# Float32 identity matmuls for the last three squarings, seven layer norms on GpSimd, and new orders throughout, in a two-layer attention and state-space kernel

## The chip, the cores and the metric

The kernel runs on one core of a Trainium2 chip. A core has five engines with an instruction queue each: TensorE (PE in the profile, its weight loads PEld), VectorE (DVE), ScalarE (ACT), GpSimd (POOL) and SyncE (SP), which here only issues DMAs. Each queue is worked off in order, and an instruction that has to wait holds up all that stand behind it. The metric is the device time of one execution in microseconds (us).

## The reference

The input `x` is 2048 rows of 512 columns in bf16. Four residual steps follow one another: attention, state-space convolution, attention, convolution, each on the layer norm of `x`. Both attention steps use the same weights, and so do both convolutions.

```python
# attention: 32 heads of 16; each row looks at 8 rows, 0, 2, ... 14 back
qkv = layernorm(x) @ wqkv
attn = softmax(q . k[s - 2w] * scale)        # masked where s - 2w < 0
x = x + (attn . v[s - 2w]) @ wo
# convolution: a kernel of 2048 taps for each of the 512 channels
P = exp(dt*A * l)                            # l = 0 .. 2047, complex, 128 states
K = einsum("dn,dnl,dn->dl", C, P, dt*B).real
x = x + irfft(rfft(layernorm(x)) * rfft(K)) + layernorm(x) * Dskip
```

## The kernel before

The work runs in six stretches, and each has an order written out by hand as a string of letters or tokens. Each letter takes the next call of its list, so the string fixes in which order every engine's queue gets its instructions.

**Front of the first attention and the taps of K (`k_gen`, ORDERK; 0 to 109 us).** The taps are built from powers of z = exp(dt A). `cur[0]` holds z as two float32 planes (real, imaginary) of 128x512. Eleven squarings give z^2 to z^2048. Squaring k takes three instructions (lines 1082 to 1090):

- `s`, `square(k)`: ACT squares both planes of `cur[k]` into `ws`.
- `i`, `double(k)`: DVE forms the new imaginary plane, 2 re im.
- `i` again, `differ(k)`: DVE subtracts the two planes of `ws`: the new real plane. `sq_z`, the tile of the result, has two buffers.

`b` (`power`, `power_neg`) makes bf16 copies of each power on ACT, for the table `B_t` (k = 0 to 2 and 8 to 11) or for `pow_t` (k = 3 to 7), which `c` completes by DMA. `C` (six DVE instructions, `c_part`) forms C times B. `M` (36 DVE instructions, `b_part`) multiplies powers to fill `B_t`; its last products need power 9 (512) and power 10 (1024). `T`, `U` and `H` build four tables `A_t`, two buffers in turn: a head (ACT copies it, for table 0 DVE) and then levels of DVE products from 256 to 4096 elements. `p` multiplies `A_t` with `B_t` on PE, and `x` copies the products to `kgs` on ACT. `G` and `w` make sine constants on ACT, among them `s_Wp` and `s_WpJ`, from which GpSimd makes the masks `Wp` and `WpJ` (line 696).

Between these stand the letters of the first attention's front. Its rows come in four blocks of 4x128 rows (`x_blk`, two buffers). `a` sums rows and squares on ACT for blocks 0 to 2, `3` takes statistics on DVE for block 3, `l` and `W` make the factor `ln_rstd` and the offset `ln_nb` of each row, and the norm itself is in place (lines 193 and 195): `y` on ACT for blocks 0 to 2, `z` on DVE for block 3. `t` transposes a block on PE (line 1194) and `e` copies it to `xnT` on ACT; `k` and `q` are the projections on PE (line 1204), `K` and `Q` their copies on ACT to `kT_ext` and `qT`.

The PSUM has eight banks. Four belong to `pst`, the pool of the first transposes, and four to the front (`la.front_psum`); when `p` starts, `pst` closes and the products `pk` take its banks.

**First attention (CORE0; to about 185 us).** `m` is the DVE product of queries and keys (`prod`, 4096 elements, 2.2 us each), `l` its sums on PE, `x`, `e`, `r`, `n`, `T` the softmax, `P` the product with the values on DVE (`pav`), `S` or `V` its sums on PE in two forms, `O` the output projection, and `a` and `f` the next norm on DVE or ACT. `A` to `H` copy the taps to `k_perm`, on the engine that KROWS names. GpSimd makes the sine arguments `g_i` and `k_perm` (lines 727 and 728).

**First convolution (ORDER0), its end with the second front (ORDERF), second attention (CORE1), second convolution (ORDER1).** `K` and `U` are the first transform step of taps and rows (copies to `a1s`), `k` and `u` the second (`kn`, `kf_sb`, `kf_nat`, `ub`), `m` the product on DVE (`t`), `y` or `Y` the first inverse step in two PE forms, `z`, `v` and `w` the last one, with the residual sum in `x_sb`. The letter behind a token names the engine of its copy: A for ACT, D for DVE. In ORDERF `h` is a layer norm's statistics on half rows, `a`, `p`, `n` the rest of the norm, `T` and `E` transposes and their copies, `P` and `Q` projections.

Of the kernel before, what the change touches and what calls it, by code (L numbers as in the profile page):

```python
# [11 lines left out]
ALU = mybir.AluOpType  # L12
# [33 lines left out]
ORDERK = """  # L46
sCiibsCbiisCiiMbMCGMiMsabiMcbiasMbbCCaGiMMTsibGGTGTicMbGsbiaTbcisbbTTTMGiiTbTiMaGsaGGTMiGacMabTl
MlMMMWMlaiMsiMayMwMiMybyaTMysteMMqatMaaMkeMadTkqMialKMMlQMkWMlaqMMcbqykTQHqUaUKqQaakUTyqUkyqUUpU
KUkyUapxUxtaUpatpeUaldHQqeUqkKUkl3TT33TQkkxpWl3KxTpTxyxTylTWTpqlkyyTqpHKkzkQzxKUtkUktezUqqeUKTkT
kQKztktkTeeKkUkUKTTkkKUUUkUxUUpxEUpkxpUkUUkpEKkKqxpkUxoxpEoKXqUokUkQUpKxpZxXxZXZ  # L50
"""
ORDER0 = """
KD KA KA KA KD KA KD KA KD KA KD kA kD kA kA kD UA KD UA UD kA UA kD UA KD UA
UD UA KD kA u UD m UA KA u UD u UD m KA u kA m m UA u u kD m m u
UA u UD kA m UA kD kA u m kA kD u kA yA m YD m u m u YA u u m u
yA m m u yA m m YA yA yD yD
"""
LATE0 = "a s t g r b m"
ORDERF = """
yA yA z01D yA z00D yA yD h00 yA h01 YA v100A v110A v102A v013A h10 a0 p0 n0G z02A v111A v101A S v112A  # L60
h02 h11 T0 E00A a1 E01A z13D p1 n1G v003A P03 Q00 h12 a2 P01 T1 E10A p2 P00 E11D n2G h03 P11 P12
P13 T2 E20A h13 a3 E21D P02 p3 n3D P22 P21 P10 T3 E30D E31D P23 P20 x1
"""
ORDER1 = """
UA UD UA UD UA UA UD UA UD UA UD u UD u u UA m u m u m UA m u m u
UD m m UA u m u m u u yA YA u m m u yD m YA m u u m m u yA
YA m yA YD w000D yA yA yD yA z03D yA w010D yA yD yA z02D v103A v113D v112D v102D v110D v100A v111D v101A
"""

CORE0 = """  # L70
vvmvvlvmvvmlvxlemvrmnlqmqvlTvqlxevqmlvmvmPvvP1rnllxS0qTmqOeVmrqP4qSl2OPPSOSOPSmPP5On3l8ml6SPCOOV
AlxSPP7eOSrObSPn9POSdOESOPSPbDadBPfaGOtFOaaawVfHSbatO
"""
CORE1 = """
0m1l2ml3mvvqqlmmlmvqqvvllxmemqvlrnvvlmxTqqlvvmqlmvPvvvvmvqlleqVPrmxqmnqSTOePlPmSOPllSPOSPrOSnOPS
mOSPOblxOSPPdeOSrffbVPdfwOnPfVOPSOSPafbOPSdafftOSafatO
"""
ROWS0 = (0, 2, 1, 3, 4, 5, 6, 7, 8, 9, 10, 11, 12, 13, 14, 15)
ROWS1 = (0, 2, 1, 3, 4, 5, 6, 7, 8, 9, 10, 11, 12, 13, 14, 15)
NCOL = (2, 2)  # L80
KROWS = "ADDAADAA"
VROWS = (*range(0, 16, 2), *range(1, 16, 2))
# [912 lines left out]
def k_gen(tc, nc, a_consts, ins, kd, la, x_v, lnst, zero, b_consts):  # L995
# [3 lines left out]
    with ExitStack() as ctx:  # L999
# [6 lines left out]
        sp = c_small.enter_context(tc.tile_pool(name="kg_small", bufs=1))  # L1006
        pst = c_psum.enter_context(tc.tile_pool(name="kg_ps_t", bufs=4, space=PSUM))
        late = {}
        iotas, a_rest = a_consts(sp)
        ident = la.c["ident"]  # L1010
        la.front_open()
        la.front_psum()
        xb, ln, lvar, xps, pps = {}, {}, {}, {}, {}
# [19 lines left out]
        def turned_by(name, rhs):  # L1033
            pt = pst.tile([P, 4, P], F32, name="pt")
            for t in range(4):
                nc.tensor.matmul(pt[:, t, :], lhsT=raw[name][:, t, :], rhs=rhs(t), start=True, stop=True)
            return pt[:].rearrange("p g q -> p q g")
# [11 lines left out]
        dtd = sp.tile([P, 4, P], BF16, name="dt_diag")  # L1049
        nc.vector.tensor_tensor(dtd[:], ident[:].unsqueeze(1).to_broadcast([P, 4, P]), pdt[:, 0, 0:4].unsqueeze(2).to_broadcast([P, 4, P]), ALU.mult)  # L1050
        by_dt, plain = (lambda t: dtd[:, t, :]), (lambda t: ident[:])
        keys()
# [19 lines left out]
        for f in head:  # L1072
            f()
        T = {name: turned_by(name, by_dt if name[0] == "C" else plain) for name in ("B_re", "B_im", "C_re", "C_im")}
        for name, copy in (("B_re", nc.scalar.copy), ("B_im", nc.scalar.copy)):
# [4 lines left out]
        nc.vector.tensor_tensor(cur[0][:, 0], a_re, cs, ALU.mult)  # L1080

        def square(k):
            nc.scalar.activation(ws[:, 0:2], cur[k][:], ACT.Square)

        def double(k):
            cur[k + 1] = sp.tile([P, 2, 4 * P], F32, name="sq_z", tag="sq_z", bufs=2)
            nc.vector.scalar_tensor_tensor(cur[k + 1][:, 1], cur[k][:, 0], 2.0, cur[k][:, 1], ALU.mult, ALU.mult)

        def differ(k):
            nc.vector.tensor_tensor(cur[k + 1][:, 0], ws[:, 0], ws[:, 1], ALU.subtract)  # L1090

        def planes(k):
            return cur[k][:].rearrange("p r (c x) -> p r c x", c=NCH)

        def power(k):
            if 3 <= k <= 7:
                nc.scalar.copy(Pw[:, :, k - 3, 1::2, :].rearrange("p c r x -> p r c x"), planes(k))
            else:
                nc.scalar.copy(Bt[:, :, :, B_L.index(1 << k), :], cur[k][:].rearrange("p r (q g) -> p r q g", g=4))

        def power_neg(k):
            nc.scalar.mul(Pw[:, :, k - 3, 2, :], planes(k)[:, 1], -1.0)

# [50 lines left out]
        def norms():  # L1154
            D2 = D * D
            for b in range(4):
                cs = slice(4 * b, 4 * b + 4)
                rstd = la.fp.tile([P, 4], F32, name="ln_rstd")
                nb = la.fp.tile([P, 4], F32, name="ln_nb")
                ln[b] = rstd, nb  # L1160
                if b < 3:
                    mean, ms = lnst["s1"][:, cs], -1.0 / D
                    msq = la.fp.tile([P, 4], F32, name="ln_msq")
                    veps = la.fp.tile([P, 4], F32, name="ln_veps")
                    lvar[b] = veps[:]
                    yield lambda: nc.vector.scalar_tensor_tensor(msq[:], mean, -1.0 / D2, mean, ALU.mult, ALU.mult)
                    yield lambda: nc.vector.scalar_tensor_tensor(veps[:], lnst["s2"][:, cs], 1.0 / D, msq[:], ALU.mult, ALU.add)
                else:
                    ag = la.fp.tile([P, 4, 2], F32, name="ln_ag")
                    lvar[b] = ag[:, :, 1]  # L1170

                    def aggr():
                        for a in range(4):
                            nc.vector.bn_aggr(ag[:, a, :], lnst["bn"][:, 12 + a, 0, :])

                    yield aggr
                    mean, ms = ag[:, :, 0], -1.0
                yield lambda: nc.vector.scalar_tensor_tensor(nb[:], mean, ms, rstd[:], ALU.mult, ALU.mult)
# [17 lines left out]
        def turned(b, d):  # L1196
            nc.scalar.copy(la.xnT[:, 2 * d:2 * d + 2, b * 512:(b + 1) * 512], xps[b, d][:].rearrange("p t a q -> p t (a q)"))

# [8 lines left out]
        def projected(kind, b, ft):  # L1207
            dst = la.kT[:, ft, 14 + b * 4:18 + b * 4, :] if kind == "k" else la.qT[b][:, ft]
            nc.scalar.copy(dst.rearrange("p a q -> p (a q)"), pps[kind, b, ft][:])  # L1209

# [59 lines left out]
        def produced(c, q8):  # L1270
            if (c, q8) == (0, 0):
                late["kgs"] = late["kgp"].tile([P, NB * 4, P], BF16, name="kgs")
            q0 = c * CH + q8 * 8
            nc.scalar.copy(late["kgs"][:, :, q0:q0 + 8].rearrange("p m (h j) -> p m h j", h=2),  # L1274
                           pks[c, q8][:, :, 0:4 * NB * 4].rearrange("p h (j m) -> p m h j", j=4))
# [38 lines left out]
        def calls(f, *args):  # L1314
            return [lambda a=a: f(*a) for a in args]

        def chain(*fs):
            for f in fs:
                yield from f

        fts = range(NDT)
        ops = dict(
            s=calls(square, *((k,) for k in range(11))), i=[f for k in range(11) for f in calls(double, (k,)) + calls(differ, (k,))],
            b=[f for k in range(12) for f in calls(power, (k,)) + (calls(power_neg, (k,)) if 3 <= k <= 7 else [])],
            C=c_part(), M=b_part(), G=steps, w=[w2_store], c=calls(power_copy, *((k,) for k in range(5))),
            a=calls(pass_stats, *((b, a, i) for b in range(3) for a in range(4) for i in range(2))), l=norms(),
            W=calls(inv_std, *((b,) for b in range(4))), y=calls(apply, *((b, a, "act") for b in range(3) for a in range(4))),
            z=calls(apply, *((3, a, "dve") for a in range(4))),
            t=calls(turn, *((b, d) for b in range(4) for d in range(2))), e=calls(turned, *((b, d) for b in range(4) for d in range(2))),
# [7 lines left out]
            x=calls(produced, *((c, j) for c in range(NCH) for j in range(CH // 8))), X=first_logits(), o=calls(lambda ft: la.front_ext(3, "act", ft), (0,), (1,), (2,)), Z=calls(lsum, (0,), (1,), (2,)))  # L1337
        ops["3"] = calls(lambda a: row_stats(nc, lnst, xb[3][:, a, :], 12 + a, "dve"), *((a,) for a in range(4)))
        ops = {key: iter(v) for key, v in ops.items()}
        for key in ORDERK.split():  # L1340
            for c in key:
                if c == "p" and c_psum is not None:
                    c_psum.close()
                    c_psum = None
                next(ops[c])()
        assert all(next(v, None) is None for v in ops.values())
        k_store()
# [231 lines left out]
```

## Time and profile before

| what | value |
| --- | --- |
| median of 3 runs | 403.36 us (403.34 to 403.40) |
| profiled execution | 402.72 us |
| its span, first to last instruction | 400.8 us |
| VectorE busy | 381.5 us (95%) |
| ScalarE busy | 326.0 us (81%) |
| TensorE busy | 320.0 us (80%) |
| GpSimd busy | 66.1 us (17%) |
| granted TensorE clock | 0.999 |

Durations in the prediction come from the one profiled execution. A line of the timeline has the start and the duration in us, the engine, the line of the kernel, the operation, the tile written and the tiles read with their shapes, and how many instructions it merges; a bracket at its end tells how long the engine was idle before it, and who released it.

### The profile page before, as it was taken

The page shows a single profiled execution, that of the slowest core. Times are in us where ns is not written, and L with a number is a line of the kernel's source. Part 1 is how long each engine was busy: PE and PEld are TensorE (multiplying, and loading weights), DVE is VectorE, ACT ScalarE, POOL GpSimd, SP SyncE. Part 2 cuts the span into 40 slices and gives each one's busy share as a digit, 9 for nine tenths or more (in the row PEclk, how much of TensorE's full clock was granted, in tenths as well). Part 3 has the DMA queues.
Part 4 walks back from the last instruction along what each step waited for, and adds up shares of the span by engine and source line. Part 5 has one row for each costly group of instructions (what it writes and reads, how often), then busy time and mean ns, then how long its engine had stood idle before and what let it go on. Part 6 is the DMA issues. An engine that isn't in the chain of part 4 may idle for free.

```text
span 400.8 us, 14761 instructions
## 1 busy us (share of the span) xinstructions
PE 320.0 (80%) x6479; PEld 227.6 (57%) x6527; DVE 381.5 (95%) x475; ACT 326.0 (81%) x565; POOL 66.1 (17%) x79
## 2 busy tenths in 40 slices
PE   3000178789999899889997889999999998998795
PEld 2000037557635567656887878643456766667785
DVE  6999999999999999999999999979999999989995
ACT  7999999786656499888999998864655788989983
POOL 9402500000299600030500002300000001000000
PEclk9999999999999999999999999999999999999999
DMA  7942820323014855285235677740063009504606
GB/s 220 395 132 31 87 65 12 83 54 94 12 39 110 216 180 152 79 296 225 101 115 206 223 270 215 263 136 2 2 169 94 3 20 404 162 2 108 213 11 205
DMA packets 62322, 54.17 MB, mean 135 GB/s; under 512 B 33869, under 2 KB 50738, under 8 KB 60978
## 3 DMA queue, kind: packets, MB, share of 16 engines
q1 hardware_dynamic: 62250, 53.22, 43.6%
q8 instruction: 51, 0.84, 0.9%
q14 instruction: 13, 0.11, 0.1%
q10 hardware_dynamic: 8, 0.00, 0.0%
HBM read 30.15 MB, written 13.24 MB: 108 GB/s over the span
## 4 chain that ended last, share of the span: by engine, by line
PE 29%; DVE 21%; issue 9%; ACT 7%; DMA 4%; SPq 1%; POOL 0%; DVEq 0%; ACTq 0%
DVE pav L465 5%; PE pq L396 5%; PE pq L501 4%; PE po L490 4%; DVE prod L340 3%; PE pq L221 3%; DVE t L849 3%; DVE t L852 3%; DVE ln_bn L148 2%; PE pb L799 2%; DMA v_ext<-v_ext 2%; PE L L352 2%; DVE a1s L788 1%; PE pb L806 1%; PE pb L883 1%
## 5 line engine op out<-in xcount | busy, mean ns | idle before, releaser
L465 DVE TENSOR_TENSOR pav<-attn,v_ext 128x4096 bf16<-128x4096 bf16 (+1 forms) x34 | 72.6, 2169 | 0.2
L340 DVE TENSOR_TENSOR prod<-qT,kT_ext 128x4096 bf16<-128x4096 bf16 x29 | 66.6, 2322 | 0.4 <-ACT qT L223 0.3
L1108 DVE TENSOR_TENSOR A_t<-A_t,pow_t 128x1024 bf16<-128x1024 bf16 (+4 forms) x46 | 37.9, 870 | 0.2
L1194 PE MATMUL pt<-ident,x_blk 128*128 128x128 bf16 x64 | 6.3, 241 | 39.6 <-ACT x_blk L193 39.6
L501 PE MATMUL pq<-wop,oT 128*128 128x512 bf16 x122 | 31.7, 379 | 3.4 <-issue 2.5
L490 PEld LDWEIGHTS <-pav 64*128 64x128 bf16 x1664 | 26.0, 95 | 13.4 <-DVE pav L465 6.0
L490 PE MATMUL po<-ident,pav 64*128 64x64 bf16 x1664 | 29.0, 190 | 4.2 <-DVE pav L465 2.3
L865 ACT CAST ub<-pb 128x1024 bf16<-128x1024 f32 x32 | 31.9, 1068 | 0.2
L398 ACT CAST v_ext<-pq 128x512 bf16<-128x512 f32 x32 | 18.8, 586 | 16.1 <-PE pq L396 16.1
L1204 PE MATMUL pp<-xnT,kT_ext 128*128 128x512 bf16 x88 | 25.3, 404 | 7.8 <-ACT qT L1209 2.8
L806 PE MATMUL pb<-a1s,w_sb 128*128 128x64 bf16 x768 | 27.3, 193 | 5.0 <-ACT a1s L788 3.1
L396 PE MATMUL pq<-wv,xnT 128*128 128x512 bf16 x120 | 29.9, 379 | 0.4
L806 PEld LDWEIGHTS <-w_sb 128*128 128x128 bf16 x768 | 24.8, 98 | 7.2 <-issue 4.8
L1194 PEld LDWEIGHTS <-x_blk 128*128 128x128 bf16 x64 | 4.7, 107 | 42.0 <-ACT x_blk L193 40.4
L788 DVE CAST a1s<-pb 128x1024 bf16<-128x1024 f32 x21 | 24.7, 1214 | 2.5 <-PE pb L799 2.2
L788 ACT CAST a1s<-pb 128x1024 bf16<-128x1024 f32 x27 | 26.4, 1043 | 0.8 <-PE pb L799 0.8
L1266 PEld LDWEIGHTS <-A_t 128*64 128x64 bf16 (+1 forms) x512 | 21.9, 103 | 4.7 <-DVE A_t L1108 0.6
L1266 PE MATMUL pk<-B_t,A_t 128*64 128x84 bf16 (+1 forms) x512 | 23.7, 201 | 1.0 <-ACT kgs L1274 0.5
L221 PE MATMUL pq<-xnT,kT_ext 128*128 128x512 bf16 x92 | 23.0, 379 | 0.2
L176 POOL TENSOR_TENSOR ln_rstd<-ln_rstd,ln_mh 128x4 f32<-128x4 f32 x2 | 4.0, 2016 | 107.4 <-DVE ln_rstd L175 107.4
L396 PEld LDWEIGHTS <-xnT 128*128 128x128 bf16 x128 | 11.7, 97 | 14.3 <-issue 1.7
L492 ACT CAST oT<-po 128x512 bf16<-128x512 f32 x26 | 14.9, 575 | 5.8 <-PE po L490 5.8
(261 smaller groups left out, 902.9 us busy)
## 6 DMA issues: line engine op xcount, KB each, us to landing
w_sb<-w_dram SPq DMA_DIRECT2D x8, 1024.0 KB, 6.8
w_dram<-xnT SPq DMA_DIRECT2D x1, 4096.0 KB
kf_ring<-kf_dram SPq DMA_DIRECT2D x13, 256.0 KB, 4.5
kf_ring<-kf_dram SPq DMA_DIRECT2D x26, 128.0 KB, 3.9
v_ext<-v_ext SPq DMA_DIRECT2D x4, 784.0 KB, 6.4
x_blk<-in_A_x_dram SPq DMA_DIRECT2D x4, 512.0 KB, 4.7
kT_ext<-in_A_wqkv_dram SPq DMA_DIRECT2D x4, 512.0 KB, 9.5
x_sb<-in_A_x_dram SPq DMA_DIRECT2D x4, 512.0 KB, 6.1
```

Source lines behind the costliest of these rows:

```text
L221: nc.tensor.matmul(pq[:], lhsT=self.wqk[:, dt, ft * P:(ft + 1) * P], rhs=self.xnT[:, dt, q * 512:(q + 1) * 512], start=(dt == 0), stop=(dt ...
L340: nc.vector.tensor_tensor(pr, self.qT[q][:, ft].unsqueeze(1).to_broadcast([P, W, 4, P]), kap, ALU.mult)
L396: nc.tensor.matmul(pp[:], lhsT=xnT[:, dt, a * P:(a + 1) * P], rhs=wv[:, dt, :], start=(dt == 0), stop=(dt == NDT - 1))
L465: nc.vector.tensor_tensor(pv[:, i], attn[:, n % 4].unsqueeze(2).to_broadcast([P, W, DH // parts, H]), vap, ALU.mult)
L490: nc.tensor.matmul(po[:, h, 0, i * nt + ft, :], lhsT=pvf[rows, i, w, ft * P:(ft + 1) * P], rhs=ident[rows, rows], start=(w == 0 and ft + i ...
L501: nc.tensor.matmul(pw[:], lhsT=oT[:, ftp, :], rhs=self.wo[:, ftp, :], start=False, stop=(ftp == NDT - 1))
L788: (self.nc.scalar.copy if eng == "act" else self.nc.vector.tensor_copy)(dst, src)
L806: nc.tensor.matmul(p2[:, j, :], lhsT=self.w2[:, ec * EC + j, :], rhs=a1s[:, ec * EC + j, :], start=True, stop=True)
L865: nc.scalar.copy(ub[:], p2)
L1108: return lambda: nc.vector.tensor_tensor(*args)
L1204: nc.tensor.matmul(pps[kind, b, ft][:], lhsT=la.wqk[:, dt, c:c + P], rhs=la.xnT[:, dt, b * 512:(b + 1) * 512], start=(dt == 0), stop=(dt = ...
L1266: nc.tensor.matmul(o, lhsT=lhs, rhs=Bt[:, ri, c * CH + ql].rearrange("p b g -> p (b g)"), start=(not half and j % 4 == 0 and ri == 0), sto ...
```

## The change

The real parts of squarings 8, 9 and 10 are formed on PE: two float32 matmuls with the identity and its negative add the squared planes into PSUM, and a third copies the imaginary plane beside them, so that `square`, `power` and `double` of the next step read `cur[k + 1]` from PSUM. `double` still writes its result to SBUF. Strings in ENGK name the engine of each norm and copy: of the 16 norms of the first front seven go to GpSimd (rows 1 to 3 of block 0, rows 0 and 3 of block 2, rows 0 and 2 of block 3), and nine stay on ACT. KROWS changes two copies from ACT to DVE. The PSUM pool of the squarings (`psz`) holds four banks until the first product; `pst` closes after the sixth `C`, and the front's pools open there. All six orders are new; ORDERF takes the second front's statistics on whole rows (`H`) in place of half rows.

```diff
+ENGK = dict(i="DDDDDDDDDDDDDDDDDPDPDP", b="AAAAAAAAAAAAAAAAA", y="AGGGAAAAGAAG", z="GAGA", e="AAAAAAAA", K="AAAAAAAAAAAAAAAA", Q="AAAAAAAA", x="AAAAAAAAAAAAAAAA")
-KROWS = "ADDAADAA"
+KROWS = "ADDADDDA"
...
-        pst = c_psum.enter_context(tc.tile_pool(name="kg_ps_t", bufs=4, space=PSUM))
+        psz = c_psum.enter_context(tc.tile_pool(name="kg_ps_z", bufs=2, space=PSUM))
+        c_turned = ExitStack()
+        pst = c_turned.enter_context(tc.tile_pool(name="kg_ps_t", bufs=4, space=PSUM))
...
+        id32 = sp.tile([P, 2, P], F32, name="ident32")
...
+        nc.scalar.copy(id32[:, 0], ident[:])
+        nc.scalar.mul(id32[:, 1], ident[:], -1.0)
...
         def double(k):
+            by_pe = ENGK["i"][2 * k + 1] == "P"
             cur[k + 1] = sp.tile([P, 2, 4 * P], F32, name="sq_z", tag="sq_z", bufs=2)
-            nc.vector.scalar_tensor_tensor(cur[k + 1][:, 1], cur[k][:, 0], 2.0, cur[k][:, 1], ALU.mult, ALU.mult)
+            ims[k + 1] = cur[k + 1][:, 1]
+            if by_pe:
+                cur[k + 1] = psz.tile([P, 2, 4 * P], F32, name="sq_p", tag="sq_p")
+            nc.vector.scalar_tensor_tensor(ims[k + 1], cur[k][:, 0], 2.0, ims[k], ALU.mult, ALU.mult)
 
         def differ(k):
-            nc.vector.tensor_tensor(cur[k + 1][:, 0], ws[:, 0], ws[:, 1], ALU.subtract)
+            if ENGK["i"][2 * k + 1] == "D":
+                nc.vector.tensor_tensor(cur[k + 1][:, 0], ws[:, 0], ws[:, 1], ALU.subtract)
+                return
+            for r in range(2):
+                nc.tensor.matmul(cur[k + 1][:, 0], lhsT=id32[:, r], rhs=ws[:, r], start=r == 0, stop=r == 1)
+            nc.tensor.matmul(cur[k + 1][:, 1], lhsT=id32[:, 0], rhs=ims[k + 1], start=True, stop=True)
...
-            W=calls(inv_std, *((b,) for b in range(4))), y=calls(apply, *((b, a, "act") for b in range(3) for a in range(4))),
-            z=calls(apply, *((3, a, "dve") for a in range(4))),
+            W=calls(inv_std, *((b,) for b in range(4))), y=calls(apply, *((b, a, by[ENGK["y"][4 * b + a]]) for b in range(3) for a in range(4))),
+            z=calls(apply, *((3, a, by[ENGK["z"][a]]) for a in range(4))),
...
+                if c == "C":
+                    parts += 1
+                    if parts == 6:
+                        c_turned.close()
+                        la.front_psum()
```

The instructions of the two programs, engine by engine, where their number differs (TensorE's two forms of sums are left out):

```
before after
   11     8  VectorE  sq_z<-ws 128x512 (differ)
    4     0  VectorE  x_blk norm
    3     5  VectorE  k_perm<-k_rl
   13    12  VectorE  xnT<-x_sb norm
   21    19  VectorE  a1s<-pb
    5     7  VectorE  kn, kf_sb, kf_nat<-pb
    4     5  VectorE  z<-pb
    4     6  VectorE  xnT<-pt
   38    22  VectorE  statistics of x_sb (32 half rows to 16 whole rows)
    5     7  VectorE  x_sb<-pb,x_sb 128x4x128
    5     3  VectorE  x_sb<-pb,x_sb 128x4x256
   12     9  ScalarE  x_blk norm
    0     2  ScalarE  ident32<-ident
    0     7  GpSimd   x_blk norm
    0     9  TensorE  sq_p<-ws or sq_z, float32
```

## The prediction

> **What bounds the kernel now.** I read the page first (busy shares, then the 40 slices), then the table of stages, then VectorE's timeline, and last the timelines of the engines that the change loads.
>
> The page's busy shares:
>
> ```profile
> PE 320.0 (80%) x6479; PEld 227.6 (57%) x6527; DVE 381.5 (95%) x475; ACT 326.0 (81%) x565; POOL 66.1 (17%) x79
> ```
>
> VectorE (DVE) idles 19.3 us of 400.8, so nearly every microsecond of DVE work is a microsecond of span. The stages (columns: length, then busy us of PE, PEld, DVE, ACT, POOL):
>
> ```profile
> 0.00:37.00 37.00, 3.16 (x25) 2.40 (x25) 32.94 (x65) 34.37 (x60) 13.75 (x42) 1.00 0.63 206
> 37.00:60.00 23.00, 9.31 (x35) 4.10 (x37) 22.93 (x38) 22.28 (x48) 7.89 (x4) 1.00 0.54 74
> 60.00:80.00 20.00, 16.60 (x263) 12.70 (x266) 19.76 (x35) 17.77 (x38) 0.00 (x0) 1.00 0.19 47
> 80.00:109.00 29.00, 27.17 (x386) 19.22 (x390) 28.80 (x35) 21.08 (x34) 1.42 (x3) 1.00 0.23 52
> ...
> 245.00:269.00 24.00, 23.45 (x221) 15.70 (x221) 20.94 (x66) 18.01 (x34) 5.03 (x6) 1.00 0.69 222
> ```
>
> The stage that the change rebuilds is the first 109 us: DVE full after 10 us, ScalarE (ACT) full up to 60 us, TensorE (PE) almost empty up to 44 us, GpSimd (POOL) free. Moving DVE and ACT work to PE and POOL looks right. What decides is who waits for the slower owners.
>
> **Work taken off DVE.** Prices are start-to-start in DVE's timeline, because busy times overlap the next start:
>
> ```profile
> 10.65 0.69 DVE L1090 TENSOR_TENSOR sq_z<-ws 128x512 f32<-128x512 f32 x1
> 11.26 0.68 DVE L1108 TENSOR_TENSOR t<-pt,in_B_im 128x512 f32<-128x512 f32 x1
> ...
> 82.18 0.41 DVE L195 TENSOR_SCALAR x_blk<-x_blk,ln_rstd,ln_nb 128x512 bf16<-128x512 bf16 x1
> 82.51 0.28 DVE L1108 TENSOR_TENSOR A_t<-A_t,A_t 128x256 bf16<-128x256 bf16 x1
> ```
>
> Three subtractions at 0.61 are 1.8 us, four norms at 0.33 are 1.3: -3.1. The doublings that now read PSUM stay at 0.6: an addition from PSUM of that size, L931, has 683 ns where L1090 from SBUF has 683.
>
> **Work moved in the other orders.** From the queues of the two programs, for DVE: two more K copies at 0.33 (+0.7), one x_sb norm fewer (-0.3), two a1s copies fewer and two spectrum copies more at 1.13 (0), one z copy more (+1.1), two 512-wide residual sums more at 0.60 for two 1024-wide fewer at 1.13 (-1.1), two transposed copies more at 0.60 (+1.2), and 16 whole-row statistics at 0.60 in place of 32 half-rows at 0.335 (-1.1). Sum +0.5.
>
> ACT in the first convolution and the second front loses two spectrum copies (0.91 each), two transposed copies (0.93), one z copy (0.91) and six small residual copies (0.54), and gains two a1s copies and four larger residual copies (0.9): about -2.4 us. It is busy there 60.9 of the 63 us from 182 to 245, where DVE idles 3.7. From 245 to 269 DVE idles 3.1. New orders can close some of these 6.8 us or open as many. I take -1.0, bounds -3 and +3.
>
> **Start of the chain.** Two copies of the identity stand ahead of the ACT copies that the first products and squaring need. A 128x128 ACT instruction steps 0.20 (F1c), so the chain starts 0.4 later; DVE idled 0.23 there already. +0.3, bounds 0 and 0.5.
>
> **The float32 matmuls.** No float32 matmul is in the trace. The nearest rows are bf16 matmuls of the same 512 columns, after a pause and in a stream:
>
> ```profile
> 49.74 1.01 PE L1204 MATMUL pp<-xnT,kT_ext 128*128 128x512 bf16 x2 [1.12 <-ACT xnT L1197]
> ...
> 60.29 1.94 PE L1204 MATMUL pp<-xnT,kT_ext 128*128 128x512 bf16 x8 [0.38 <-ACT kT_ext L1209]
> ```
>
> That is 0.22 to 0.5 us a pass. One pass is the low end; a float32 value needs three bf16 values, so three paused passes, 1.5 us, are the high end. I take 1.3, since PE is nearly idle there. Squaring 8 is covered: ACT has about 4.3 us of other work between the squares, against three matmuls of 1.3. Squaring 9 is not: double(10) reads the PSUM pair, whose imaginary copy starts only after double(9), and just two B_t instructions (0.33 each) stand between them on DVE. 1.3 and 0.1 of signalling less 0.66: +0.7, bounds 0 and 0.95. Squaring 10 is needed late.
>
> By the Trainium skill ("FP8 and Floating Point Precision", TensorE Precision Notes) true float32 takes four passes: 2.0 us paused, a wait of 1.4, and the sum would be 0.7 higher. No run here shows it.
>
> **Block 0 on GpSimd.** ACT made all four norms of block 0; now rows 1 to 3 are POOL's. In POOL's queue they stand behind the four masks Wp and WpJ, and the masks wait for two sines on ACT. Before:
>
> ```profile
> 37.16 2.89 POOL L696 TENSOR_TENSOR Wp<-s_Wp,aux 64x64 bf16<-64x64 f32 x2 [22.44 <-ACT s_Wp L677]
> 40.11 5.11 POOL L696 TENSOR_TENSOR WpJ<-s_WpJ,aux 64x64 bf16<-64x64 f32 x2
> ...
> 190.22 3.02 POOL L195 TENSOR_SCALAR xnT<-x_sb,ln_rstd,ln_nb 128x512 bf16<-128x512 bf16 x4 [15.18 <-DVE ln_nb L183]
> ```
>
> A POOL norm takes 0.75 while DVE reads PSUM, as at 190. Beside DVE's back-to-back two-input SBUF products POOL is held: the third mask ran from 40.11 to about 43.2 and ended at a tiny DVE instruction. Walked with the old durations, ACT's new queue reaches the sines at 41.9 (36.8 before). The wait of double(10) lets the masks finish near 46, and norm 1 near 47. Then DVE runs 4.7 us of B_t and A_t products without a gap, up to about 51.8. If norms 2 and 3 slip in at once, they end near 48.5; if they are held, near 53.3.
>
> Who waits: PE's transposes need all four rows (five of them after the last norm took 0.71). ACT's next instruction, the xnT copy (0.9), waits for PE, and behind it stand a square sum (0.6) and the bf16 copy of power 10 (0.93), which DVE needs at 51.8 for its 1024 product. So DVE goes on 3.3 us after the last norm: at 51.8 if that ended by 48.5, at 56.6 if at 53.3. Before, that copy ran ahead of the transposes:
>
> ```profile
> 44.76 1.05 ACT L1099 CAST B_t<-sq_z 128x1024 bf16<-128x1024 f32 x1
> ...
> 48.70 0.99 ACT L1197 COPY xnT<-pt 128x1024 bf16<-128x1024 bf16 x1
> ```
>
> Bounds 0 and 4.8; both kinds of row exist, so I take the middle, +2.4.
>
> **Four later norms, and the port.** The other four POOL norms fall among statistics and small products; ACT and PE had waits there (kgs, kT_ext: 3.1 and 4.3 us). POOL's presence lengthens DVE: where eight POOL L728 instructions ran (108 to 137 us) DVE's rows are longer than their steps of 2.2 (plus 0.08 at a row's end) and 0.68 allow:
>
> ```profile
> 109.60 7.42 DVE L340 TENSOR_TENSOR prod<-qT,kT_ext 128x4096 bf16<-128x4096 bf16 x3
> ...
> 122.51 1.09 DVE L443 TENSOR_TENSOR ex<-ex,rs 128x1024 bf16<-128x1024 bf16 x1
> ```
>
> That is 0.7 and 0.4, with 0.4 each in two rows after: 1.9 us for eight, 0.25 each. Four norms: +1.0; bounds 0 (all in DVE's gaps) and 2.9 (seven at 0.41).
>
> **Table heads.** The head of table 2 on ACT was done 5 us before DVE used it; DVE now uses it before, not after, two 4096-wide products (4.4 us), on an ACT that is late. +0.7, bounds 0 and 2.
>
> **Sum.** -3.1 + 0.5 - 1.0 + 0.3 + 0.7 + 2.4 + 1.0 + 0.7 = +1.5 us. On the profiled execution, 402.72 us (span 400.8 and 1.9 around it), this gives 404.2. The median of the runs lies 0.64 above the profiled one, so I forecast 404.9 as the median. About 0.2% (0.8 us) is what a measurement tells from no change.
>
> **Rivals.** *POOL gets its turns* (the other side). Norms 2 and 3 run between DVE's products at 0.75 to 0.85 each, as L195 does at 190 and 248. Then the block 0 wait and the table head term vanish: 1.5 - 2.4 - 0.7 = -1.6, or -2.0 with a one-pass matmul: 401.4. It decides if the last norm of block 0 ends before the power 10 copy is due, 48.5 on my walk. For it: prod rows that gave POOL turns. Against it: the masks.
>
> *POOL is held throughout*: 4.8 for block 0, 2 for the table head, 0.95 for double(10), no gain elsewhere: 1.5 + 2.4 + 1.3 + 0.25 + 1.0 = +6.4, 409.8. For it: masks of 2.5 us. Against it: DVE's stalls set POOL free.
>
> *Each POOL norm makes DVE stand for its full length.* Norms start at the next boundary, so block 0 is late by 0.5 at most, but seven times 0.77 is 5.4: 1.5 - 1.9 - 0.7 + 4.4 = +3.3, 406.7. Against it: 0.25 measured, and masks that passed several boundaries without a turn. This is the exclusive lock of the Trainium skill ("SBUF — State Buffer", two separate sides: whoever starts first holds the shared ports for the whole instruction); the trace agrees on POOL held by DVE, and not on a turn at the next boundary.
>
> *The later orders decide.* They close 3 of the 6.8 idle us from 182 to 269 and not 1: with half the block 0 wait, 1.5 - 2.0 - 1.2 = -1.7, 401.7.
>
> *The parts cancel*, or PE's and POOL's help never reaches DVE's queue: 403.4.
>
> **How the numbers follow.** Forecast 0.40, POOL gets its turns 0.26, POOL held 0.14, full-length lock 0.06, later orders 0.06, cancel 0.08. Faster 0.26 + 0.06 = 0.32, same 0.08, slower 0.60. The forecast's own range is 403.6 to 407. The whole range takes in both faster cases with their unknown port cost, and part of the held case: 400.8 to 408.5.
>
> **What would show it.** Right: in the profile after, POOL's x_blk norms of block 0 last over 1.5 us in the mean, DVE idles at double(10) on PE, and at the 1024-power B_t product on ACT, at 45 to 57 us; DVE's busy time falls by 2 to 3 us. Wrong: DVE without idle before 109 us, or idle that moved to the later stages; then the port, or the orders, were the larger term.

## The result and the profile after

The changed kernel takes 406.60 us in the median (404.50 to 407.86), before takes 403.35 on the same chip: a ratio of 1.0076 (95% interval 1.0058 to 1.0093), 3.25 us slower. The profiled execution of after took 407.86 us (span 406.1), 1.3 us above its median, and before's lies 0.6 below its own. So the two profiles differ by 5.3 us of span where the medians differ by 3.25, and the differences of stretches below come out too large in sum.

The page's busy shares after, and the granted clock in 40 slices:

```profile
PE 336.9 (83%) x6353; PEld 238.5 (59%) x6401; DVE 379.0 (93%) x456; ACT 321.1 (79%) x558; POOL 62.8 (15%) x86
...
PEclk9999688999999999999999899999999999999898
```

VectorE's work fell by 2.5 us, and its idle time rose from 19.3 to 27.1. The clock's row, all nines before, has dips. Which stretches the idle time lies in, by events that both kernels have on VectorE (us):

| from, to | before | after |
| --- | --- | --- |
| start, first `prod` | 109.60 | 110.35 |
| to the end of the last `pav`, first attention | 75.77 | 75.12 |
| to the first `prod` of the second attention | 83.75 | 86.88 |
| to the first `a1s` on VectorE, second convolution | 87.85 | 87.65 |
| to the end | 43.83 | 46.10 |

The rebuilt front is 0.75 longer, the first convolution with the second front 3.1, the last stretch 2.3. The table of stages after (columns as in the prediction, the last three the granted clock, the DMA share and GB/s), and below it the last of these rows before:

```profile
37.00:60.00 23.00, 13.74 (x42) 5.95 (x42) 21.62 (x36) 18.72 (x41) 5.40 (x7) 0.81 0.52 68
60.00:80.00 20.00, 18.83 (x241) 13.23 (x244) 17.95 (x29) 18.34 (x40) 1.56 (x2) 0.88 0.16 42
...
222.00:245.00 23.00, 18.81 (x530) 17.46 (x528) 18.75 (x27) 19.16 (x21) 0.34 (x1) 0.93 0.77 273
```

```profile
222.00:245.00 23.00, 19.84 (x662) 18.21 (x662) 21.41 (x32) 22.08 (x25) 0.35 (x1) 1.00 0.66 232
```

VectorE idles 1.4 us from 37 to 60 and 2.1 from 60 to 80 (0.1 and 0.2 before), and 4.3 from 222 to 245 (1.6 before). In each of these stages the clock is below 1 after.

First the place that the prediction walked through. TensorE's timeline after, then VectorE's, GpSimd's and ScalarE's:

```profile
33.52 3.78 PE L1106 MATMUL sq_p<-ws,ident 128*128 128x512 f32 x4 [25.95 <-ACT ws L1091]
...
39.51 1.98 PE L1106 MATMUL sq_p<-ws,ident 128*128 128x512 f32 x4 [1.11 <-ACT ws L1091]
44.93 2.08 PE L1107 MATMUL sq_p<-sq_z,ident 128*128 128x512 f32 x2 [3.44 <-DVE sq_z L1099]
```

```profile
44.20 0.68 DVE L1099 SCALAR_TENSOR_TENSOR sq_z<-sq_p,sq_z 128x512 f32<-128x512 f32 x1
...
47.05 0.69 DVE L1099 SCALAR_TENSOR_TENSOR sq_z<-sq_p,sq_z 128x512 f32<-128x512 f32 x1 [1.38 <-PE sq_p L1107]
```

```profile
42.12 2.48 POOL L698 TENSOR_TENSOR Wp<-s_Wp,aux 64x64 bf16<-64x64 f32 x2 [28.15 <-ACT s_Wp L679]
44.66 0.72 POOL L698 TENSOR_TENSOR WpJ<-s_WpJ,aux 64x64 bf16<-64x64 f32 x2
45.49 2.32 POOL L197 TENSOR_SCALAR x_blk<-x_blk,ln_rstd,ln_nb 128x512 bf16<-128x512 bf16 x3
```

```profile
48.69 1.01 ACT L1221 COPY xnT<-pt 128x1024 bf16<-128x1024 bf16 x1
...
50.21 1.01 ACT L1120 CAST B_t<-sq_p 128x1024 bf16<-128x1024 f32 x1
```

A float32 matmul is two records here (x4 for two matmuls). The one at 44.93 took 2.08 us, at a granted clock of 0.50; the two at 39.51 took 0.99 each, at 1.00. VectorE waits 1.38 us at `double(10)`. Of the three norms of block 0 that GpSimd makes, 0.77 each, two lie in that wait and the third beside `double(10)` itself, which reads PSUM. The four masks ahead of them had ended at 45.38, before the wait began: the last three took 0.29 to 0.38 us each from 44.31 on, two of them beside `double(9)`, which now reads PSUM too (VectorE's first row). The copy of power 10 is done at 51.2, VectorE needs it at 53.5: nobody waits for block 0.

The second wait of the front, which the prediction gave to a late ScalarE, is this one (VectorE, then TensorE):

```profile
70.98 4.90 DVE L1132 TENSOR_TENSOR A_t<-A_t,pow_t 128x256 bf16<-128x256 bf16 x4 [1.77 <-ACT A_t L1249]
```

```profile
57.54 1.33 PE L1228 MATMUL pp<-xnT,kT_ext 128*128 128x512 bf16 x4 [2.58 <-ACT qT L1233]
60.33 1.86 PE L1228 MATMUL pp<-xnT,kT_ext 128*128 128x512 bf16 x4 [1.46 <-ACT kT_ext L1233]
61.99 2.58 PE L1290 MATMUL pk<-B_t,A_t 128*128 128x84 bf16 x32
```

The head of table 2 needs a buffer that the products of table 0 still read, and these run at half speed: 32 take 2.58 us, where 32 took 1.49 before:

```profile
64.46 1.49 PE L1266 MATMUL pk<-B_t,A_t 128*128 128x84 bf16 x32
```

The third wait is in the first convolution, at a copy of VectorE, first before, then after:

```profile
224.62 1.23 DVE L788 CAST kn<-pb 128x1024 bf16<-128x1024 f32 x1 [0.79 <-DMA kf_dram<-kn]
```

```profile
226.08 1.22 DVE L790 CAST kn<-pb 128x1024 bf16<-128x1024 f32 x1 [2.83 <-DMA kf_dram<-kn]
```

The chain of waits that led to it after, from 222 us:

```profile
223.05 0.59 SPq L836
223.63 0.04 issue
223.68 2.28 DMA kf_dram<-kn
...
226.08 0.10 DVE kn L790
```

VectorE's copy of a spectrum stood 2.83 us until an earlier spectrum had been stored and its buffer was free; the store itself had waited on SyncE behind two swapped loads. ScalarE and then TensorE stood too, and the clock was 0.66 from 225 to 230.

### The profile page after: what moved, and what is told of

The parts are those of the page before. It is cut to its first block, busy times and chain, and to the rows that moved or that the text cites. A ratio compares the mean times of both kernels' runs of the same rounds, so it can differ in the third digit from the quotient of the medians.

```text
span 406.1 us, 14498 instructions
## 1 busy us (share of the span) xinstructions
PE 336.9 (83%) x6353; PEld 238.5 (59%) x6401; DVE 379.0 (93%) x456; ACT 321.1 (79%) x558; POOL 62.8 (15%) x86
## 4 chain that ended last, share of the span: by engine, by line
PE 35%; DVE 20%; issue 8%; ACT 7%; DMA 1%; SPq 1%; DVEq 0%; ACTq 0%
DVE pav L467 5%; PE pq L398 5%; PE pq L503 4%; DVE prod L342 4%; PE po L492 4%; PE pq L223 3%; ACT ub L867 2%; PE po L482 2%; PE pp L282 2%; PE pb L808 2%; PE pb L885 2%; PE L L354 2%; ACT xnT L790 2%; DVE t L854 2%; DVE a1s L790 2%
## 5 line engine op out<-in xcount | busy, mean ns | idle before, releaser
L808 PE MATMUL pb<-a1s,w_sb 128*128 128x64 bf16 x768 | 29.9, 200 | 6.7 <-ACT a1s L790 1.9
L808 PEld LDWEIGHTS <-w_sb 128*128 128x128 bf16 x768 | 27.2, 103 | 9.0 <-issue 7.7
L492 PEld LDWEIGHTS <-pav 64*128 64x128 bf16 x1536 | 24.0, 95 | 12.7 <-DVE pav L467 5.7
L1106 PE MATMUL sq_p<-ws,ident 128*128 128x512 f32 x12 | 8.0, 801 | 27.3 <-ACT ws L1091 27.1
L492 PE MATMUL po<-ident,pav 64*128 64x64 bf16 x1536 | 27.1, 190 | 3.5 <-DVE pav L467 1.3
L790 ACT CAST a1s<-pb 128x1024 bf16<-128x1024 f32 x29 | 28.2, 1045 | 1.5 <-PE pb L801 1.5
L790 DVE CAST a1s<-pb 128x1024 bf16<-128x1024 f32 x19 | 22.5, 1216 | 2.7 <-PE pb L801 2.6
L225 ACT CAST qT<-pq 128x512 bf16<-128x512 f32 x24 | 14.1, 586 | 9.5 <-PE pq L223 9.1
L1106 PEld LDWEIGHTS sq_p<-ws,ident 128*128 128x128 f32 x12 | 2.9, 258 | 30.9 <-ACT ws L1091 28.3
L509 ACT ACTIVATE x_sb<-pq 128x512 bf16<-128x512 f32 x24 | 14.2, 594 | 7.0 <-PE pq L503 6.9
```

The lines of the kernel that those rows point to most:

```text
L492: nc.tensor.matmul(po[:, h, 0, i * nt + ft, :], lhsT=pvf[rows, i, w, ft * P:(ft + 1) * P], rhs=ident[rows, rows], start=(w == 0 and ft + i ...
L790: (self.nc.scalar.copy if eng == "act" else self.nc.vector.tensor_copy)(dst, src)
L808: nc.tensor.matmul(p2[:, j, :], lhsT=self.w2[:, ec * EC + j, :], rhs=a1s[:, ec * EC + j, :], start=True, stop=True)
```

## The experiments

Each is given beside before on the same chip; medians in us, ratio with its 95% interval.

**Front or later orders.** `front_new` is after with ORDER0, ORDERF, ORDER1, CORE0, CORE1 and KROWS of before; `later_new` is before with these six of after.

```diff
-KROWS = "ADDADDDA"
+KROWS = "ADDAADAA"
...
```

> The changed front of the first attention (float32 matmuls, norms on GpSimd, the new ORDERK) with all later orders and KROWS of before. Theory of the front (the prediction's own: double(10), block 0 and the table head cost more than the 3.1 us taken off VectorE): about 2.5 us above before, 405.9, and its two stages up to the last pav of the first attention 2 to 3 us longer than before's 185.4. Theory of the later orders (the profiles up to the last pav of the first attention differ by 0.1 us, the loss lies behind it): 403.4, within 0.5 of before.

> The front of before, unchanged, with the changed kernel's ORDER0, ORDERF, ORDER1, CORE0, CORE1 and KROWS. Theory of the front: these orders give a little back, 402.4 to 403.4. Theory of the later orders: the whole loss is here, 406 to 407.5, with VectorE waiting over 2 us for the store of kn in the first convolution.

`front_new`: 405.89 beside 403.28, ratio 1.0068 (1.0044 to 1.0093), +2.6. `later_new`: 405.32 beside 403.28, 1.0047 (1.0030 to 1.0065), +2.0. Each theory had half. The front alone costs about what the prediction's sum gave it (+2.0), and the later orders cost too, where the prediction had a gain. Together they cost 3.25 and not 4.6; the intervals are too wide to call that more than a hint. In `front_new` the first stretch is 1.2 us longer than before (110.79), the rest of its loss is spread over stretches whose instructions and orders are those of before (45.11 in the last); why, no run settled.

**One convolution's order back.** `conv1st_old` is after with ORDER0 and ORDERF of before, `conv2nd_old` after with ORDER1 of before.

> The changed kernel with ORDER0 and ORDERF (first convolution and second front) of before; all else as changed. Theory of the front: no faster than the changed kernel, 406.6 or more. Theory of the later orders, first convolution: the stage from the last pav of the first attention to the first prod of the second goes from 86.9 back to about 83.8 us, and the median falls by about 3, to 403.5.

> The changed kernel with ORDER1 (second convolution) of before; all else as changed. In the profile of the changed kernel this last stage was 2.3 us longer than before, with the granted clock at 0.66 in a stretch of 5 us. If the new ORDER1 is the reason, the median falls by 1 to 2.3 us, to 404.3 to 405.6; if the clock in that one execution is, it stays at 406.6 within 0.5.

`conv1st_old`: 406.34, ratio 1.0092 (1.0058 to 1.0126). The stretch fell as expected (86.9 to 84.85) and the wait for the store was gone, but the second attention took 90.0 us in place of 87.7, and the median stayed. In its trace TensorE paused 1.71 us inside one group of `po` sums ("issue", nothing that the profile shows), and VectorE's `pav` waited 1.5 for it. A pause in one execution can't account for the median of six, though. The median is what the theory of the front expected, the shorter stretch what the other theory did; this run doesn't decide between them. `conv2nd_old`: 406.44, 1.0074 (1.0055 to 1.0093); the last stretch has before's 43.8, and the median stayed too. ORDER1 alone isn't the loss; whether it has a share of a microsecond stays open.

**The first convolution in before.** `conv1st_new` is before with ORDER0 and ORDERF of after.

> Before with the changed kernel's ORDER0 and ORDERF alone (first convolution and second front). If the first convolution is where later_new lost its 2.0 us: 1.5 to 2.5 us above before, the stage from the last pav of the first attention to the first prod of the second 86 to 87 us (83.8 before), with VectorE's wait for the store of kn and a lower clock behind it. If the loss lies in ORDER1 and CORE1: within 0.5 of before.

404.60 beside 403.36, ratio 1.0024 (1.0003 to 1.0045): slower, by 1.2 and not 1.5 to 2.5. The stretch is 85.98, VectorE waits 2.9 for the store of `kn`, and the clock falls behind it. Over all profiles: with the new ORDER0 and no added buffers this wait is 1.5 to 4.1 us, with the old one 0 to 1.2; `xnT` waits 2.3 for the transposes with the new ORDERF and 0.8 to 0.9 with the old.

**Norms back.** `norms_back` is `front_new` with

```diff
-y="AGGGAAAAGAAG", z="GAGA"
+y="AAAAAAAAAAAA", z="DDDD"
```

> front_new (the changed front, all later orders of before; 405.9) with its seven GpSimd norms back on their old engines: five on ScalarE, two on VectorE (of the four that left VectorE, two are ScalarE's in both). Theory of the prediction (block 0 on GpSimd costs 2.4, the other four and the port 1.0; the norms taken off VectorE save 0.7): about 2.7 us faster, 403.2. Theory from the trace of the changed kernel (the three norms of block 0 ran in 2.3 us, inside VectorE's wait at double(10), and nobody waited for them): no faster, and with 0.7 us more on VectorE and 3.5 more on ScalarE slower, 406 to 408.

403.80 beside 402.72, ratio 1.0034 (1.0015 to 1.0053): +1.1, where `front_new` had +2.6. So it is 1.5 faster, against the reading that the norms are free. The expectation counted two norms for VectorE; the edit gives it all four of block 3, two of them from ScalarE, so that every norm is where before has it. With four, the prediction's terms give 2.1 us (2.4 + 1.0 - 1.3) in place of 2.7. But no wait for block 0 stands in either trace. VectorE's busy time in the front is 102.96 with its four norms and 102.78 without them: less 1.3 for the four, GpSimd's seven norms lengthen VectorE's work by about 1.1. Work and port nearly cancel, then. Of the gain, 0.6 us stand in the first stretch (110.19 in place of 110.79), where the wait for the head of table 2 is 1.3 in place of 2.0; the rest lies in later stretches with the same orders, and no run settled why.

**Squarings back.** `squares_back` is `front_new` with

```diff
-i="DDDDDDDDDDDDDDDDDPDPDP"
+i="DDDDDDDDDDDDDDDDDDDDDD"
```

> front_new with the three squarings' subtractions back on VectorE (no float32 matmul; the norms stay on GpSimd, the orders stay). VectorE gets 1.8 us of work back and loses the wait of double(10), 1.4 us. By this count: 406.3, no faster. Theory of TensorE's clock (the early float32 matmuls and the pause after them leave the granted clock at 0.5 to 0.8 from 45 to 65 us, TensorE's products for tables 0 and 1 come late, and VectorE waits 2.0 us for the head of table 2): that wait goes too, 404.3, and the clock's row shows 1.0 from 45 us.

410.43 beside 402.72, ratio 1.0182 (1.0164 to 1.0199): 7.7 slower. Neither theory had it: the wait for the head of table 2 stays too, at 1.6 us, and 32 products take 2.53 (at 68.78) though no float32 matmul is left and the clock's row reads 1.00 there. GpSimd's timeline in this kernel, then ScalarE's, then VectorE's:

```profile
45.04 8.75 POOL L698 TENSOR_TENSOR WpJ<-s_WpJ,aux 64x64 bf16<-64x64 f32 x2
53.90 2.27 POOL L197 TENSOR_SCALAR x_blk<-x_blk,ln_rstd,ln_nb 128x512 bf16<-128x512 bf16 x3
```

```profile
56.97 1.01 ACT L1221 COPY xnT<-pt 128x1024 bf16<-128x1024 bf16 x1 [8.81 <-PE pt L1218]
...
58.50 1.03 ACT L1120 CAST B_t<-sq_z 128x1024 bf16<-128x1024 f32 x1
```

```profile
44.92 0.68 DVE L1099 SCALAR_TENSOR_TENSOR sq_z<-sq_z 128x512 f32<-128x512 f32 x1
...
59.57 0.69 DVE L1132 TENSOR_TENSOR B_t<-B_t 128x1024 bf16<-128x1024 bf16 x1 [6.28 <-ACT B_t L1120]
```

VectorE's products run without a gap until 53.3. GpSimd is held in the first of two small masks for 8.40 us, to 53.44, and the norms start only when VectorE has nothing left. From the last norm (56.2) it takes 3.4 us by the transposes, the copy to `xnT`, a square sum and the copy of power 10 until VectorE goes on: the walk of the prediction (3.3 us), with every station, but in a kernel where no float32 matmul makes VectorE pause. So the two parts of the change need each other. What the masks need is not the wait at `double(10)`, before which they had ended in after, but `double(9)`, VectorE's first row above, when it reads PSUM. In all ten profiles where it does (`sq_p`), a mask beside it takes 0.28 to 0.29 us; in the four where it reads SBUF alone, the mask that starts beside it takes 1.99 to 8.40.

**TensorE kept busy.** `pe_warm` is `front_new` with fifteen bf16 matmuls that nobody reads.

```diff
+def keep_warm(n):
+    if "warm" not in late:
+        late["warm"] = psz.tile([P, 2, 4 * P], F32, name="warm", tag="sq_p")
+    for j in range(n):
+        nc.tensor.matmul(late["warm"][:, j % 2], lhsT=ident[:], rhs=la.xnT[:, 0, 0:512], start=True, stop=True)
...
+ops["J"] = calls(keep_warm, (10,), (5,))
-MqiMlkeqWkMlMbMQMkMyMkHdKaqqKTp
+MqiMlkeqWkJMlMbMQMkMyMkHdKaJqqKTp
```

> front_new with fifteen extra bf16 matmuls of 512 columns, whose result nobody reads, in TensorE's two pauses at 55.0 (ten) and 58.9 us (five). They add work and take none away. Theory of TensorE's clock: the granted clock stays near 1 from 57 to 65 us, 32 pk products take 1.5 us and not 2.6, VectorE's wait of 2.0 us for the head of table 2 shrinks below 0.7, and the median falls by 1.3 to 2, to about 404.3. Theory that ScalarE's queue alone is late there: no gain, 405.9 or up to 0.5 more.

401.67 beside 402.72, ratio 0.9976 (0.9945 to 1.0008); 3.7 us better than `front_new`, each against before on its own chip, and more than expected. The windows of after, then of `pe_warm` (PE's busy time is the second number, the clock is the third from the end):

```profile
56.00:60.00 4.00, 1.33 (x4) 0.44 (x4) 4.00 (x8) 2.81 (x6) 0.00 (x0) 0.77 0.01 5
60.00:64.00 4.00, 3.67 (x31) 2.43 (x31) 3.86 (x8) 3.87 (x9) 0.00 (x0) 0.50 0.01 4
```

```profile
56.00:60.00 4.00, 4.00 (x20) 1.83 (x19) 4.00 (x8) 2.81 (x6) 0.00 (x0) 1.00 0.00 0
60.00:64.00 4.00, 3.69 (x43) 2.28 (x43) 3.86 (x8) 4.00 (x10) 0.00 (x0) 1.00 0.02 4
```

and the products of table 0 in `pe_warm`:

```profile
61.23 1.48 PE L1293 MATMUL pk<-B_t,A_t 128*128 128x84 bf16 x32
```

Adding TensorE work took VectorE's wait for the head away whole; the first stretch is 108.71, 2.1 less than in `front_new` and 0.9 less than before. This is the causal run for the clock: ScalarE's queue is the same. The other 1.6 us lie in stretches whose instructions are the same, and stay unexplained. The page "TensorE: Matmul & The Clock Gate" of the Trainium skill (Part 1) says that the clock halves after an idle window of some 3.4 us and needs as long a busy one to recover, by windows that run freely; the trace agrees in kind, though here a shorter pause was enough: the clock is 1.00 up to 58.1 us and 0.50 from there, after the pause of 2.58 us and ahead of the one of 1.46.

Such a dip is not the changed front's alone. `later_new` and `conv1st_new` have before's front, and their clock falls to 0.50 at 59.0 and 60.1 us, for 3.4 us, after pauses of 2.01 and 2.33; before's own profile has a pause of 1.89 there and no dip. VectorE does not wait for the head of table 2 in any of the three.

**double(10) later.** `double_later` is `front_new` with

```diff
-ayyiMMsyMMTMte
+ayyMMsyMMiTMte
```

> front_new with double(10) behind the four 1024-wide products that follow it on VectorE (one letter of ORDERK moved). Theory that its wait is plain loss: the 1.4 us go, 404.5. Theory of the held GpSimd: the wait is what let GpSimd make the three norms of block 0 at 0.8 us each; without it they are held behind VectorE's products, last over 1.5 us in the mean, and TensorE, ScalarE and then VectorE wait for them: 405.5 to 407, with a new wait of VectorE at 50 to 57 us.

403.08 beside 402.72, ratio 1.0004 (0.9980 to 1.0027): 2.2 better than `front_new`. The wait is gone, and GpSimd is held as the second theory said:

```profile
45.40 4.50 POOL L197 TENSOR_SCALAR x_blk<-x_blk,ln_rstd,ln_nb 128x512 bf16<-128x512 bf16 x3
```

That is 1.5 us for a norm in place of 0.77, and two VectorE products beside them take 1.06 and 1.09 in place of 0.68. But they end at 49.9, the copy of power 10 at 53.2, and VectorE comes for it at 53.28: no new wait. The float32 matmuls of squaring 10 moved later too, so that TensorE's pause before the projections shrank to 0.29 us and the products ran at full clock (first stretch 108.51); this run therefore holds both gains and does not price the 1.4 us alone. It does show that the norms of block 0 can do without the wait; their masks had ended at 45.30, again beside `double(9)`.

**Clock cure in the whole changed kernel.** `after_warm` is after with the fifteen matmuls of `pe_warm`.

> The changed kernel, all its later orders included, with the fifteen unread bf16 matmuls of pe_warm in TensorE's two pauses. Theory of TensorE's clock: VectorE's wait for the head of table 2 (1.8 us) goes here too, the stage up to the first prod falls from 110.4 to about 108.7 us, and the median by 2 to 4, to 1.0 us on either side of before. Theory that the later orders hold the whole loss: no gain, about 3.3 us above before.

407.67 beside 403.36, ratio 1.0110 (1.0078 to 1.0143): 4.3 above before, a miss. The front did what was expected (108.73), and the first convolution took it back: 88.24 in place of 86.88, with 4.1 us of waiting for stores of `kn`. So the 1.6 us won in the front were mostly waited for at the shortage of buffers behind it.

**More buffers.** `after_spare` is `after_warm` with two more spectrum buffers.

```diff
+            more = self.c_mid.enter_context(tc.tile_pool(name="b0_more", bufs=2, reuse_waits="tile"))
+            self.free += [more.tile([P, DQG, EC], BF16, name="kf_more")[:] for _ in range(2)]
```

> after_warm (the changed kernel with its later orders, and unread matmuls in TensorE's pauses of the front; 4.3 us above before) with two more spectrum buffers in the first convolution, taken from free SBUF. If VectorE's waits of 1.5 to 4.1 us for the store of kn come from the new ORDER0 running out of free spectrum buffers, so that a copy must wait until an earlier spectrum has been stored: the wait falls below 1 us, the stage from the last pav of the first attention to the first prod of the second goes from 88.2 to 85 to 86, and the time falls by 2 to 3.5, to 1 to 2 us above before. If the stores are late for another reason (SyncE's queue, the DMA rate): the wait stays over 2 us and the time within 0.7 of after_warm.

403.83 beside 402.86, ratio 1.0013 (0.9991 to 1.0036): from 4.3 above before to 1.0, which the interval can't tell from no change. No wait for a store of `kn` is left, the stretch fell from 88.24 to 83.84, below the 85 to 86 expected, and the clock stays at 1. That the new ORDER0 runs out of buffers is shown; the wait of 2.3 us for the transposes, which is ORDERF's, stayed.

**The better version.** `best_a` is `front_new` with `double(10)` later, unread matmuls (6 and 4) in the two pauses, and in squaring 9 two more float32 matmuls into the plane that its copy then overwrites.

```diff
+            for r in range(2 if k == 9 else 0):
+                nc.tensor.matmul(cur[k + 1][:, 1], lhsT=id32[:, 0], rhs=ws[:, r], start=True, stop=True)
```

> front_new with both cures: double(10) behind four products, unread matmuls in TensorE's pauses (six and four of bf16 at 57 us, two of float32 between the sums and the copy of squaring 9), and all later orders of before. If both waits come from TensorE's pauses and its clock: TensorE stays at full clock from about 38 us, the float32 copy of squaring 9 takes 1.0 us and not 2.1, VectorE waits less than 0.5 us at double(10) and at the head of table 2, and the time is 2 us below before (about 401 where before is 403) in every run, where double_later and pe_warm each had a group of runs 3 us slower. If their slower runs have another cause: half of its runs lie above before again.

The groups meant there: the times of `pe_warm` reach from 400.58 to 404.85, those of `double_later` from 400.72 to 405.48.

401.80 beside 403.36, ratio 0.9965 (0.9946 to 0.9984): faster than both kernels. The float32 copy of squaring 9 takes 1.13 us, and neither wait is left (0.2 us at the head of table 2). Its times reach from 400.57 to 403.92, though: not every run is 2 us below before, and what makes single executions slower is not settled. TensorE is not at full clock from 38 us either; the row reads 0.50 from 48.0 to 54.7 us.

## Why the prediction was right, and where it was not

The forecast was 404.9 with a range of 400.8 to 408.5, slower at 0.60; 406.6 is slower, in the range and in the forecast's own (403.6 to 407). But several terms were wrong and cancelled, and that the time came out near is partly luck. The figure nearest to the result, 406.7, was that of the rival "each POOL norm makes DVE stand for its full length", and its mechanism did not occur: the seven norms lengthened VectorE's work by about 1.1 us and not by 5.4. Step by step:

- **Work off VectorE, -3.1, and the port, +1.0.** Right, each by itself: VectorE's busy time in the front fell from 104.93 to 102.83. `squares_back` gives 1.8 for the three subtractions, as counted, and `norms_back` about 1.1 for the port.
- **Start of the chain, +0.3.** Nothing: VectorE idles no more from 9 to 33 us than before (0.03 beside 0.30).
- **double(10), +0.7.** 1.38, beyond its bound of 0.95. The mis-sized number is the float32 matmul, 1.3 taken from three paused passes. Measured are 2.08 us at a clock of 0.50 and 1.02 at 1.00. The sentence on the Trainium skill ("FP8 and Floating Point Precision", four passes) had 2.0 us and a wait of 1.4: the trace agrees with it, where the bound from bf16 rows failed.
- **Block 0 on GpSimd, +2.4.** 0. The rival "POOL gets its turns" was right here, at 0.77 a norm. The step that failed is the walk's order of events. It let the wait of `double(10)` free the masks, near 46, and one norm, and put the other two behind VectorE's products. It did not ask what `double(9)` and `double(10)` leave free now that they read PSUM, though it named a norm's price beside such reads (the rows at 190 lay beside them for a third of their time). In the trace the masks got through beside `double(9)` and ended at 45.38, two norms ran in the wait, which was twice as long as forecast, and the third beside `double(10)`: the last ended at 47.81, ahead of the walk's own limit of 48.5. The priced mechanism is real, as `squares_back` shows at 6.3 us of waiting. By the Trainium skill ("SBUF — State Buffer", two separate sides) whoever starts first holds the ports; there the mask held for 8.40 us ended 0.15 us after VectorE had stopped, and the trace agrees that GpSimd is blocked. Why that mask got no turn between eleven instructions of VectorE, and the norms of `double_later` did, no run shows.
- **Table head, +0.7.** 1.77, inside the bounds of 0 to 2, for another reason: not a late ScalarE but TensorE at half clock after its pauses. The prediction has no term for the clock. `pe_warm` shows it.
- **Front in sum.** The forecast terms give -3.1 + 0.3 + 0.7 + 2.4 + 1.0 + 0.7 = +2.0. The same terms as measured give -2.1 + 0 + 1.38 + 0 + 1.77 = +1.05, and the first stretch grew by 0.75 in after and by 1.2 in `front_new`. The forecast was a microsecond too high; that `front_new` measured +2.6 comes from its loss in later stretches, for which there was no term. That agreement is luck.
- **Later orders, -1.0 and +0.5 of moved work.** `later_new` +2.0. This term has the wrong sign. The moved work has it too, with no harm: behind the first stretch VectorE is busy for 276.2 us, 276.6 before. The relief of ScalarE came (VectorE's waits for `ln_rstd` and `kT_ext` in the second front, 1.1 and 0.7 us, are gone), but idle time from the last `pav` to the second attention rose from 6.4 to 9.7 us: 2.7 more for stores of `kn`, 1.4 more for the transposes. The prediction counted copies by engine and not the buffers that they need, and its bound of +3 just failed in this profile (+3.3).

The rival "later orders decide" had the right place and the wrong direction. Of the signs that were to show the prediction right, the idle at `double(10)` and VectorE's lower busy time (2.5 us) occurred; norms of over 1.5 us and an idle at the 1024-power product did not. And a sign that it was wrong, "idle that moved to the later stages", did occur.

## What to carry to other kernels

Work moved to an idle engine brings its rhythm with it: a queue that starts and pauses runs at a lower clock just when its results are due, and a few unread matmuls in the pauses can be worth more than the work saved. When an order is written anew, count the buffers that each copy takes and the stores that give them back, since a microsecond won ahead of a dry pool is only waited for later. And where one engine is held up beside another, look at what the other reads: a mask on GpSimd took 0.29 us beside a doubling from PSUM, and 8.40 us beside the same doubling and the products behind it from SBUF.

## What the runs showed of the hardware

- TensorE's clock reads 1.00 from 52 to 56 us in before's windows, yet there five 512-column matmuls take 2.43 us from 52.77, and six take 1.57 from 55.43. In `best_a` it reads 0.50 from 10.5 to 37.7 us, and two float32 matmuls at 33.53 take 3.78 us, as in after, where it reads 1.00. In `squares_back` the 32 products of 2.53 us at 68.78 stand under 1.00 too. So in the first stretch of an execution the row has to be read with the durations.
- A float32 matmul of 128x512 takes 2.08 us at a granted clock of 0.50 and 1.02 at 1.00, some four times a bf16 matmul in before's rows just named (0.49 and 0.26).
- TensorE twice paused inside a group of sums for nothing that the profile shows: 1.71 us in `conv1st_old`, 2.38 in `after_spare` (178.70 us). Pauses of this size hide effects of a microsecond in a single profile.
